# Attention and two MLPs on one core: the score buffer of queries 256 to 575 as two tiles of two banks, with a new table for the order

## The chip, the cores and the metric

The kernel runs on one core of a Trainium2 chip. The metric is the device time of one execution in microseconds. The engines are TensorE (PE; PEld are its weight loads), VectorE (DVE), ScalarE (ACT), GpSimd (POOL, nearly unused here) and SyncE (SP), whose queue issues every transfer. PE writes its products to PSUM, eight banks of 512 numbers per partition; DVE and ACT read them there.

## The reference

Three stages, all in 32-bit numbers. First causal attention by blocks of 64 (4 batches, 8 heads, 576 positions, 64 numbers per head):

```python
scores = scale * np.matmul(q, k.transpose(0, 1, 3, 2))
mask = block_i >= block_j
scores = np.where(mask, scores, -1000000000.0)
scores = scores - np.max(scores, axis=-1, keepdims=True)
attn = np.exp(scores)
attn = attn / (np.sum(attn, axis=-1, keepdims=True) + 1e-09)
return np.matmul(attn, v).astype(np.float32)
```

Its output is seen as 2304 tokens of 512 numbers. The first MLP is `h = x @ w_in` (512 to 2048), softplus, `g @ w_out` (2048 to 512). The second is `h = x @ w_in` (512 to 1024), h times softmax(h), a layer norm, and `ln @ w_out` (1024 to 512).

## The kernel before

**Precision.** Most operands are split into a high and a low part (`do_hi`/`do_lo`, `qk_hi`/`qk_lo`, `do_gh`/`do_gl`), and a product is three matmuls: high by high, high by low, low by high.

**Units of work.** `UnitA` (16 of them) is attention for queries 0 to 255 of one batch and two heads. `Piece` loads and splits one block of weights. `Pair` is two blocks of 128 hidden units of the first MLP for one chunk of 256 tokens: 24 matmuls into a tile `hp`, softplus on ACT and DVE (`abs`, `exp`, `ln`, `stt`, `do_gh`, `do_gl`), 24 matmuls into `acc`. `UnitC` (16 of them) is attention for queries 256 to 575 of one batch and two heads. `Tok` is the second MLP for 128 tokens (`h` and `op` are its matmul outputs).

**UnitC.** Its scores come in three parts: i = 0 (queries 256 to 383, 384 keys, two heads), i = 1 (queries 384 to 511, 512 keys, two heads) and i = 2 (the last 64 queries of both heads, 576 keys). They stand in one PSUM tile `S` of four banks: i = 0 in banks 0 and 1, i = 1 in banks 2 and 3, i = 2 again in banks 0 and 1 (`BANKS`, line 75). `mm_both` computes i = 0 and 1 in one go, `mm_qk(2)` comes when the exponentials of i = 0 are done. For each part `mask` writes the masked block (L466), `max` takes the row maximum (L471) and `exp` the exponentials with their sums (L480, one instruction per head). The exponentials are 32-bit; `split` copies their 16-bit halves apart (L243 on ACT, L245 on DVE), `tr` transposes them by a transfer (L511), and `merge` puts the halves together in `ps` (L521). `pv` multiplies `ps` with v into bank 3 of `S`; `scale` multiplies the result with the reciprocal sums (L537), and `x_hi`/`x_lo` (L243 or L245, L544) split it for the first MLP. `pv` and what follows of a unit are planned by `tail` while the next unit's scores are under way, so the product of unit n stands in the queues behind the scores of unit n+1.

**Order.** Every step is a task of a planner, `Plan`, with a duration, a rank and the tasks that it waits for; a task that can run on ACT or DVE names both. The planner lists the tasks engine by engine with a clock of its own; ranks are changed by the numbers in `OFF` (per step) and `RANK` (per kind of unit). The program is then emitted in that order and not reordered. Which semaphore waits an instruction gets is decided after that, from the tiles that it reads and writes. Every matmul but the transposes is recorded at L237.

Of the kernel before, what the change touches and what calls it, by code (L numbers as in the profile page):

```python
# [20 lines left out]


OFF = {
    "Pair.a": -30572.7, "Pair.abs": 25914.2, "Pair.b": -12790.1, "Pair.do_gh": -42748.1, "Pair.do_gl": -11944.0,
    "Pair.evac": -75046.1, "Pair.exp": -224132.0, "Pair.ln": -58821.8, "Pair.store": 28299.8, "Pair.stt": -51658.7,
    "Piece.bits0": -37390.9, "Piece.bits0@P0": 71539.5, "Piece.bits1": 159910.0, "Piece.bits1@P0": -41379.4,
    "Piece.do_hi": 106001.0, "Piece.do_hi@P0": 54788.8, "Piece.do_hi_g": -165029.0, "Piece.do_lo": 218994.0,
    "Piece.do_lo@P": -242194.0, "Piece.do_lo@P0": -14117.0, "Piece.do_lo_g": -38167.0, "Piece.load": 118853.0,
    "Piece.load@P0": -53132.4, "Piece.signed": 7535.9, "Piece.signed@P0": -56998.9, "Tok.a": -51047.8,
    "Tok.aggr": -41912.4, "Tok.bm": 27290.6, "Tok.center": -145283.0, "Tok.exp": 132540.0, "Tok.ln_hi": 136461.0,  # L30
    "Tok.ln_lo": 51440.0, "Tok.load": -208829.0, "Tok.logexp": -32647.3, "Tok.max": -40011.4, "Tok.merge": -254456.0,
    "Tok.mul": 16809.9, "Tok.o_evac": 16072.7, "Tok.small1": 16163.9, "Tok.small2": 138442.0, "Tok.split": 28685.9,
    "Tok.split_hi": -133834.0, "Tok.split_lo": -100488.0, "Tok.stats": -115234.0, "Tok.store": 248643.0,
    "Tok.tr": -134887.0, "Tok.x_hi": -156806.0, "Tok.x_lo": 115109.0, "UnitA.copy": -106614.0,
# [14 lines left out]
    "UnitC.den2": 150139.0, "UnitC.exp": 48708.5, "UnitC.load_qk": 26177.4, "UnitC.load_v": 7244.7,  # L49
    "UnitC.mask": -46322.9, "UnitC.max": -100744.0, "UnitC.merge": 34385.8, "UnitC.merge4": 216201.0,  # L50
    "UnitC.mm_both": -75275.5, "UnitC.mm_qk": 98914.6, "UnitC.norm": 45831.4, "UnitC.pv": 35917.7,
    "UnitC.qk_hi": -133419.0, "UnitC.qk_lo": -2441.9, "UnitC.rs_load": 47376.0, "UnitC.rs_store": -119437.0,
    "UnitC.scale": -84530.8, "UnitC.split": 35598.0, "UnitC.tr": -112828.0, "UnitC.x_hi": 94264.4,
    "UnitC.x_lo": -3061.1, "UnitC.xx": 34443.5,
}
RANK = {
# [4 lines left out]
}  # L61
MARGIN = {
    "PE": 600.0, "ACT": 100.0, "DVE": 100.0, "POOL": 100.0,
# [8 lines left out]

QA = (slice(0, 128), slice(128, 384))
MASKED = -8.0e9
BANKS = (slice(0, 2), slice(2, 4), slice(0, 2))

WC = (384, 512, 576)

# [149 lines left out]
def body(ctx: ExitStack, tc: tile.TileContext, qk, qkA, vP, vA, w1, w2, u1, u2, gln, out):  # L228
# [127 lines left out]
    class UnitC:  # L356
# [6 lines left out]
        def plan(self, prev, opened):  # L363
            p1, p2 = at_of(prev, len(prev) - 1), at_of(prev, len(prev) - 2)

            def g(u, *names):
                return [getattr(u, x) for x in names] if u else []

            self.t_qk = add("SP", dma_ns(128 * 3840), -12, self.load_qk, [opened] + g(p1, "t_ql"), DMA_LAT)
            self.t_qh = add({"ACT": act_ns(960), "DVE": dve_ns(960, .52)}, None, -6, self.qk_hi, [self.t_qk] + g(p1, "t_mm"))  # L370
            self.t_ql = add("DVE", dve_ns(960), -6, self.qk_lo, [self.t_qh])
            self.t_tr, self.t_mg, self.t_exp = [None, None, None], [[], [], []], {}
            mm01 = add("PE", 1614, 0.0, self.mm_both, [self.t_ql] + ([p1.t_exp[2, 0], p1.t_exp[1, 0]] if p1 else []) + g(p2, "t_xn"))
            for i, w in enumerate(WC):
                r, heads = 7.0 * i, ((0, 1), (1, 0), (0,))[i]
                if i < 2:
                    t = add("DVE", 140, r, partial(self.mask, i), [mm01])
                else:
                    self.t_mm = t = add("PE", 797, r, partial(self.mm_qk, 2), [mm01, self.t_exp[0, 0], self.t_exp[0, 1]])
                t = add("DVE", dve_ns(w * len(heads)), r, partial(self.max, i), [t])  # L380
                e = []
                for j in heads:
                    e.append(add("ACT", 250 + .833 * w, r, partial(self.exp, i, j), [t] + e + (p1.t_mg[i] if p1 else [])))
                    self.t_exp[i, j] = e[-1]
                if i == 1 and p1:
                    p1.tail([self.t_exp[1, 1]])
                cols, back = w * len(heads), [p1.t_tr[i]] if p1 else []
                n = [add({"ACT": 100 + .833 * cols, "DVE": 75 + .52 * cols}, None, r, partial(self.split, i, k), e + back) for k in range(2)]
                self.t_tr[i] = add("SP", 300 + 1.6 * cols, r, partial(self.tr, i), n, 2600.0)
            for i, w in enumerate(WC):  # L390
                r, cols = 7.0 * i + 4, w * (2 if i < 2 else 1)
                self.t_mg[i].append(add("DVE", 75 + 1.04 * cols, r, partial(self.merge, i), [self.t_tr[i]] + g(p1, "t_pv")))
                if i == 2:
                    self.t_mg[i] += [add({"ACT": 230, "DVE": 215}, None, r, partial(self.merge4, j), [self.t_tr[i]] + g(p1, "t_pv")) for j in range(2)]
            self.t_v = add("SP", dma_ns(327680), -8, self.load_v, [opened, self.t_qk] + g(p1, "t_pv", "t_v"), DMA_LAT)
            t = chain("DVE", 15, ((70, self.den0), (80, self.den1), (190, self.den2)), list(self.t_exp.values()) + g(p2, "t_rs"))
            self.t_rs = add("SP", 420, 15, self.rs_store, [t], 2400.0)
            self.t_rr = add("SP", 1000, 16, self.rs_load, [self.t_rs] + (p2.t_x if p2 else []), 2500.0)
            self.p1, self.group = p1, plan.group
            prev.append(self)  # L400
# [43 lines left out]

        def scores(self, i):

            return state["S"][:, BANKS[i], 0:WC[i] if i < 2 else WC[2] // 2]

        def mm_qk(self, i):
            S, w = self.scores(i), WC[i]  # L450
# [74 lines left out]
            copy(e, state["p4"].bitcast(U16)[64 * j:64 * j + 64].rearrange("p (q two) -> p q two", two=2), src)  # L525

        def pv(self):
            o, ps = state["S"][:, 3], state["ps"]
            for t in range(4):
                q0 = 0 if t < 3 else 128  # L530
                for j in range(2):
# [2 lines left out]

        def scale(self):
            self.xn = self.r
            DVE.tensor_mul(self.xn, state["S"][:, 3, 0:NB], self.r)  # L537

        def x_hi(self, c, off, done, w, e):
            copy(e, xt_of(c)[:, 0, self.pr, off:off + w], self.xn[:, done:done + w])  # L540
# [256 lines left out]
    def open_b():  # L797
# [1 line left out]
        right[0] = ExitStack()  # L799
        state["pat"] = right[0].enter_context(pool("atB", "right"))  # L800
        q = right[0].enter_context(pool("qaB", "right", space=PSUM))
        state["S"] = q.tile([128, 4, 512], F32, name="S")
        state["dC"] = [[state["pat"].tile([128, 32], F32, name=f"d{x}{i}") for x in "CT"] for i in range(2)]
        for d, _ in state["dC"]:
            DVE.memset(d, 1.0)
# [328 lines left out]
```

## Time and profile before

| | us |
|---|---|
| three runs, median (lowest, highest) | 785.98 (784.9, 786.38) |
| the profiled execution, its own time | 783.34 |
| its span from the first to the last instruction | 781.5 |
| PE busy, in the span | 734.6 |
| DVE busy, ACT busy | 577.6, 414.7 |

The span has three stages: UnitA with the weights up to 183.7 us, UnitC from there to about 440 us, and what is left of the first MLP with the second one up to the end. Pairs run beside all of the first two stages. The granted TensorE clock was 0.998 of the full 2.4 GHz in the mean.

### The profile page before, as it was taken

To read this page: it belongs to the slowest core of one execution; us is meant where nothing else is said; L and a number is where in the kernel's file an instruction comes from. 1 tells how busy PE (TensorE), PEld (TensorE's weight loads), DVE (VectorE), ACT (ScalarE), POOL (GpSimd) and SP (SyncE) were. 2 spreads that over 40 slices of the span, in tenths; PEclk is the share of its full clock that TensorE was granted. 3 is DMA by queue.
4 is the path that set the end of the run, shared out by engine and by line. 5 is a ranking of instruction groups with operands and counts; after the bars stand their busy time and mean duration, and the time that the engine had idled before them with its cause. 6 is when DMAs were issued, how large, how long until landed. Compare 5 with 4: busy or idle time off the path is not lost.

```text
span 781.5 us, 13790 instructions
## 1 busy us (share of the span) xinstructions
PE 734.6 (94%) x5336; PEld 654.3 (84%) x5336; DVE 577.6 (74%) x1219; ACT 414.7 (53%) x874; POOL 0.7 (0%) x6
## 2 busy tenths in 40 slices
PE   7799999999988888889879999999999999999998
PEld 5688889998777777778768999999999888888887
DVE  5998894367877788878867555424698999988882
ACT  5776765474557667766756455333463333323331
POOL 0000000000000000000000000000000000000000
PEclk9999999999999999999999999999999999999999
DMA  6754630212776777677676332002514443443323
GB/s 226 250 201 162 203 128 2 74 44 66 151 157 131 151 151 172 148 147 159 151 143 105 91 116 101 28 1 77 193 55 90 121 98 98 109 95 94 66 72 79
DMA packets 152673, 91.87 MB, mean 118 GB/s; under 512 B 122272, under 2 KB 135840, under 8 KB 152608
## 3 DMA queue, kind: packets, MB, share of 16 engines
q1 hardware_dynamic: 152608, 90.99, 46.0%
q8 instruction: 42, 0.69, 0.4%
q14 instruction: 23, 0.19, 0.1%
HBM read 51.91 MB, written 9.70 MB: 79 GB/s over the span
## 4 chain that ended last, share of the span: by engine, by line
PE 69%; DVE 14%; ACT 10%; DMA 4%; issue 3%; SPq 0%; ACTq 0%; DVEq 0%
PE hp L237 16%; PE acc L237 16%; PE op L237 13%; PE h L237 13%; PE S L237 8%; ACT eC L480 5%; DVE mC L471 4%; DMA raw<-in_w_dram 4%; PE R L237 2%; DVE a L314 2%; ACT hl L243 1%; DVE w L324 1%; DVE gl L758 1%; DVE t L750 1%; ACT t L741 1%
## 5 line engine op out<-in xcount | busy, mean ns | idle before, releaser
L237 PE MATMUL hp<-xt,w 128*128 128x256 f32 x1728 | 217.1, 281 | 0.1
L237 PEld LDWEIGHTS hp<-xt,w 128*128 128x128 f32 x1728 | 206.8, 189 | 6.3 <-issue 5.4
L237 PE MATMUL acc<-gh,w 128*128 128x256 f32 x768 | 146.3, 282 | 0.0
L237 PEld LDWEIGHTS acc<-gh,w 128*128 128x128 f32 x768 | 122.5, 190 | 2.9 <-issue 2.9
L237 PE MATMUL acc<-gl,w 128*128 128x256 f32 x384 | 107.7, 281 | 0.0
L237 PE MATMUL h<-u,w 128*128 128x512 f32 x432 | 100.6, 389 | 0.0
L237 PE MATMUL op<-w,w2w 128*128 128x512 f32 (+1 forms) x456 | 100.3, 378 | 0.0
L237 PEld LDWEIGHTS op<-w,w2w 128*128 128x128 f32 x456 | 82.5, 188 | 16.0
L237 PEld LDWEIGHTS h<-u,w 128*128 128x128 f32 x432 | 80.8, 188 | 16.5
L480 ACT ACTIVATE eC<-S,mC 128x384 f32<-128x384 f32 (+2 forms) x80 | 52.1, 653 | 72.5 <-DVE mC L471 28.6
L741 ACT ACTIVATE t<-hp 128x512 f32<-128x512 f32 x72 | 42.9, 596 | 83.7 <-PE hp L237 71.2
L750 DVE SCALAR_TENSOR_TENSOR t<-hp,t 128x512 f32<-128x512 f32 x72 | 49.3, 684 | 48.8 <-ACT t L747 47.9
L237 PEld LDWEIGHTS acc<-gl,w 128*128 128x128 f32 x384 | 72.6, 189 | 0.0
L471 DVE TENSOR_REDUCE mC<-S 128x2 f32<-128x768 f32 (+2 forms) x48 | 45.5, 975 | 9.1 <-ACT eC L480 5.0
L237 PE MATMUL S<-ps,v 128*64 128x320 f32 (+1 forms) x256 | 34.6, 412 | 18.6 <-DVE mC L471 14.2
L243 ACT ACTIVATE hl<-eC 128x576 uint16<-128x576 uint16 (+2 forms) x62 | 49.6, 829 | 0.8
L758 DVE TENSOR_TENSOR gl<-t,gh 128x512 fp32r<-128x512 f32 x72 | 49.1, 682 | 1.0 <-ACT gh L243 0.2
L237 PE MATMUL acc<-gh,w2w 128*128 128x256 f32 x256 | 48.4, 281 | 0.0
L744 ACT ACTIVATE t<-t 128x512 f32<-128x512 f32 x72 | 45.5, 633 | 1.5
L521 DVE COPY ps<-eC 128x1536 uint16<-128x1536 uint16 (+2 forms) x48 | 45.5, 947 | 1.1 <-DMA eC<-hl 1.0
L747 ACT ACTIVATE t<-t 128x512 f32<-128x512 f32 x72 | 45.3, 629 | 1.1
L237 PEld LDWEIGHTS S<-ps,v 128*64 128x64 f32 x256 | 16.9, 136 | 33.7 <-DVE mC L471 16.4
(173 smaller groups left out, 1050.0 us busy)
## 6 DMA issues: line engine op xcount, KB each, us to landing
raw<-in_w_dram SPq DMA_DIRECT2D x32, 512.0 KB, 4.3
qkC<-in_qk_dram SPq DMA_DIRECT2D x16, 480.0 KB, 4.0
raw_u<-in_u_dram SPq DMA_DIRECT2D x11, 512.0 KB, 3.5
v<-in_vP_dram SPq DMA_DIRECT2D x16, 320.0 KB, 3.1
x2s<-stg SPq DMA_DIRECT2D x18, 256.0 KB, 2.8
xr<-x2s SPq DMA_DIRECT2D x18, 256.0 KB, 3.2
qkA<-in_qkA_dram SPq DMA_DIRECT2D x16, 256.0 KB, 3.5
out_dram<-ob SPq DMA_DIRECT2D x15, 256.0 KB, 2.0
```

Source lines behind the costliest of these rows:

```text
L237: PE.matmul(out, lhsT, rhs, start=start, stop=stop, skip_group_check=True)
L243: ACT.activation(out, a, AF.Copy)
L314: DVE.scalar_tensor_tensor(out=self.a, in0=self.raw[:, :, 0], scalar=29, in1=self.a, op0=ALU.logical_shift_right, op1=ALU.bitwise_or)
L324: DVE.tensor_sub(self.lo, self.af, self.hi)
L471: DVE.tensor_reduce(out=self.m[:, i:4:2] if i < 2 else self.m[:, 4:5], in_=self.scores(i), axis=AX.X if i < 2 else AX.XY, op=ALU.max, nega ...
L480: ACT.activation(e, sc, AF.Exp, bias=self.m[:, c:c + 1], accum_out=self.den[:, d:d + 1])
L521: DVE.tensor_copy(dst, src)
L741: ACT.activation(self.t, self.hp, AF.Abs)
L744: ACT.activation(self.t, self.t, AF.Exp, scale=-1.0)
L747: ACT.activation(self.t, self.t, AF.Ln, bias=1.0)
L750: DVE.scalar_tensor_tensor(out=self.t, in0=self.hp, scalar=0.0, in1=self.t, op0=ALU.max, op1=ALU.add)
L758: DVE.tensor_sub(self.gl, self.t, self.gh)
```

## The change

The four-bank tile becomes two tiles of two banks, `S0` and `S1`. The banks are used as before: i = 0 and i = 2 in `S0`, i = 1 in `S1`, the product with v in the second bank of `S1`. `tail` of the unit before now hangs on the second exponential of i = 1 (head 0) and not on the first (head 1). All numbers in `OFF` and `RANK` are new (two rows of each are shown); the planner itself is the same.

```diff
 OFF = {
-    "Pair.a": -30572.7, "Pair.abs": 25914.2, "Pair.b": -12790.1, "Pair.do_gh": -42748.1, "Pair.do_gl": -11944.0,
+    "Pair.a": -37545.4, "Pair.abs": 40935.4, "Pair.b": -12936.9, "Pair.do_gh": -72836.8, "Pair.do_gl": 135125.0,
...
 RANK = {
-    "U2": (1044770.0, 6788.0), "Tok": (617171.0, 18564.5),
+    "U2": (1063100.0, 9138.15), "Tok": (672137.0, 5865.35),
...
-BANKS = (slice(0, 2), slice(2, 4), slice(0, 2))
...
                 if i == 1 and p1:
-                    p1.tail([self.t_exp[1, 1]])
+                    p1.tail([self.t_exp[1, 0]])
...
         def scores(self, i):
-            return state["S"][:, BANKS[i], 0:WC[i] if i < 2 else WC[2] // 2]
+            return state["S"][i % 2][:, :, 0:WC[i] if i < 2 else WC[2] // 2]
...
         def pv(self):
-            o, ps = state["S"][:, 3], state["ps"]
+            o, ps = state["S"][1][:, 1], state["ps"]
...
-            DVE.tensor_mul(self.xn, state["S"][:, 3, 0:NB], self.r)
+            DVE.tensor_mul(self.xn, state["S"][1][:, 1, 0:NB], self.r)
...
-        state["S"] = q.tile([128, 4, 512], F32, name="S")
+        state["S"] = [q.tile([128, 2, 512], F32, name=f"S{i}") for i in range(2)]
```

The lines below `BANKS` stand one line higher afterwards (L471 becomes L470). In the whole program DVE has 1241 instructions in place of 1219, and ACT 690 in place of 712 without the reads of sums; among what moved to DVE are 16 casts of `gh`. From the first mask of a UnitC to its last `scale` DVE has 427 in place of 414.

The first place is DVE in the middle of the UnitC stage, from the masks of one unit's scores to the maximum of i = 2 (128x1); the words in brackets name what an instruction waits for. Before:

```order
L466 MEMSET S_2238 64x2x64 [waits PE_49]
L466 MEMSET S_2238 64x2x64 [waits DVE_49]
L471 TENSOR_REDUCE mC_3152<-S_2238 128x2 [waits DVE_49]
L471 TENSOR_REDUCE mC_3152<-S_2238 128x2
L521 COPY ps_2252<-eC1_2246 128x2x4x256 [waits DMAHW2_49]
L245 COPY hl0_2248<-eC0_2245 128x768 [waits Activation_49]
L521 COPY ps_2252<-eC2_2247 128x8x128 [waits DMAHW4_49]
L750 SCALAR_TENSOR_TENSOR t_3132<-hp0_130,t_3132 128x512
L432 TENSOR_SCALAR qkh_3214<-qkC_3076 128x384 [waits DMAHW1_49,PE_49]
L433 CAST qkh_3214<-qkC_3076 128x576
L471 TENSOR_REDUCE mC_3152<-S_2238 128x1 [waits Activation_49]
```

The same stretch on DVE after the change, for the next unit but one:

```order
L465 MEMSET S0_2238 64x2x64 [waits PE_49]
L465 MEMSET S1_2239 64x2x64 [waits PE_49]
L470 TENSOR_REDUCE mC_3366<-S0_2238 128x2 [waits DVE_49]
L470 TENSOR_REDUCE mC_3366<-S1_2239 128x2 [waits DVE_49]
L520 COPY ps_2253<-eC2_2248 128x8x128 [waits DMAHW2_49]
L244 COPY hl0_2249<-eC0_2246 128x768 [waits Activation_49]
L244 COPY hl0_2249<-eC0_2246 128x768
L244 COPY hl1_2250<-eC1_2247 128x1024 [waits Activation_49]
L244 CAST gh_3424<-t_3282 128x512 [waits PE_49]
L757 TENSOR_TENSOR gl_3435<-t_3282,gh_3424 128x512 [waits DVE_49]
L470 TENSOR_REDUCE mC_3366<-S0_2238 128x1 [waits PE_49]
```

Each mask now waits for PE by itself, each maximum of i = 0 and 1 for its own mask, and the maximum of i = 2 for PE and no longer for ACT. The large merge has moved ahead of the masks; splits of i = 0 and a cast of `gh` stand where it was.

The second place is PE, from the scores of i = 2 (288 columns) over the product with v (`S<-ps,v`, `S<-p4,v`) to what follows it; `hp` are matmuls of a Pair. Before:

```order
L237 MATMUL S_2238<-qkh_3214 128x288 x2
L237 MATMUL S_2238<-qkl_3215,qkh_3214 128x288 x2
L237 MATMUL S_2238<-qkh_3214,qkl_3215 128x288 x2
L237 MATMUL hp1_131<-xt_2584,w1_2_99 128x256 x12
L237 MATMUL S_2238<-ps_2252,v_3298 64x320 x6
L237 MATMUL S_2238<-ps_2252,v_3298 64x192 x2
L237 MATMUL S_2238<-p4_2253,v_3298 128x64
L237 MATMUL hp1_131<-xt_2584,w1_3_100 128x256 x12
```

After, in a unit at about the same place:

```order
L236 MATMUL S0_2238<-qkh_3262 128x288 x2
L236 MATMUL S0_2238<-qkl_3263,qkh_3262 128x288 x2
L236 MATMUL S0_2238<-qkh_3262,qkl_3263 128x288 x2
L236 MATMUL S1_2239<-ps_2253,v_3325 64x320 x6
L236 MATMUL S1_2239<-ps_2253,v_3325 64x192 x2
L236 MATMUL S1_2239<-p4_2254,v_3325 128x64
L236 MATMUL hp0_130<-xt_2639,w1_4_101 128x256 x12
L236 MATMUL hp0_130<-xt_2639,w1_5_102 128x256 x12
L236 MATMUL S0_2238<-qkh_3437 128x384 x2
```

A product now writes `S1` and scores of i = 2 write `S0`. In every other unit nothing stands between them any more, and 48 in place of 36 matmuls of Pairs stand ahead of them; in the units between it is 36 and 12, as before everywhere. A unit has 72 matmuls of Pairs in its round in both orders.

## Rows read from the trace of the kernel before

**Rows 1.** The page: span; busy time and its share by engine.

```profile
span 781.5 us, 13790 instructions
PE 734.6 (94%) x5336; PEld 654.3 (84%) x5336; DVE 577.6 (74%) x1219; ACT 414.7 (53%) x874; POOL 0.7 (0%) x6
```

**Rows 2.** Windows (first column): length, busy of PE, PEld, DVE, ACT, POOL; clock; DMA.

```profile
0.00:183.70 183.70, 170.91 (x1450) 154.47 (x1450) 137.08 (x347) 115.90 (x283) 0.70 (x6) 1.00 0.42 140
183.70:440.00 256.30, 225.44 (x1799) 195.43 (x1800) 200.62 (x415) 166.30 (x361) 0.00 (x0) 0.99 0.68 142
440.00:778.25 338.25, 338.21 (x2094) 304.38 (x2088) 239.91 (x457) 131.99 (x230) 0.00 (x0) 1.00 0.33 87
285.58:316.31 30.73, 27.17 (x216) 23.23 (x217) 24.61 (x53) 21.46 (x47) 0.00 (x0) 1.00 0.72 164
```

**Rows 3.** Waits of PE, 184 to 440: who waited for whom; us, times, longest.

```profile
PE S L237 <- ACT eC L480: 15.5, 16, 3.0
PE S L237 <- DVE mC L471: 14.2, 11, 1.5
```

**Rows 4.** The chain that ended last, 284 to 332: start, us, what.

```profile
285.58 2.53 PE S L237 x18
...
292.51 0.18 DVE S L466
...
292.97 2.10 DVE mC L471 x2
...
295.14 0.67 ACT eC L480 x2
...
298.30 1.34 ACT eC L480 x4
...
299.67 0.77 DVE mC L471
...
300.48 2.53 PE S L237 x18
...
316.31 2.53 PE S L237 x18
```

**Rows 5.** Timeline, 284 to 304: start, us, engine, operation, idle before and releaser.

```profile
288.15 0.74 ACT L480 ACTIVATE eC<-S,mC 128x576 f32<-128x576 f32 x1 [2.32 <-PE S L237]
...
296.95 0.53 PE L237 MATMUL S<-qkh 128*128 128x288 f32 x2 [0.24 <-ACT eC L480]
...
297.85 0.28 PE L237 MATMUL acc<-gh,w2w 128*128 128x256 f32 x1
...
303.91 0.49 DVE L537 TENSOR_TENSOR rC<-S,rC 128x320 f32<-128x320 f32 x1 [1.75 <-ACT eC L480]
```

**Rows 6.** The chain that ended last, elsewhere: one block of a Pair; scores.

```profile
290.99 1.44 PE S L237 x12
...
446.34 2.83 PE acc L237 x24
```

**Rows 7.** Groups by line and shape: the cast of `gh` on either engine.

```profile
L245 DVE CAST gh<-t 128x512 fp32r<-128x512 f32 x43 | 18.2, 423 | 7.0 <-PE acc L237 4.9 <-PE R L237 1.7
...
L243 ACT ACTIVATE gh<-t 128x512 fp32r<-128x512 f32 x29 | 18.1, 625 | 3.9 <-PE acc L237 2.3 <-DVE t L750 1.3
```

**Rows 8.** Waits of DVE, 285.58 to 316.31: us, times, longest.

```profile
DVE rC L537 <- ACT eC L480: 1.7, 1, 1.7
DVE hl L245 <- ACT eC L480: 1.4, 2, 0.7
DVE dC L483 <- ACT eC L480: 1.1, 1, 1.1
...
DVE S L466 <- PE S L237: 0.5, 1, 0.5
```

**Rows 9.** Timeline of SP: the large transpose of one unit: start, us.

```profile
302.02 3.58 SPq L511 DMA_TRANSPOSE eC<-hl  x1
```

**Rows 10.** Window after PE's longest wait: length, PE busy, clock, DMA, GB/s.

```profile
405.00:410.00 5.00, 2.81 (x12) 0.72 0.81 98
```

More of the change, by code (lines that the diff above doesn't have):

```diff
@@ L23 @@
 OFF = {
-    "Pair.a": -30572.7, "Pair.abs": 25914.2, "Pair.b": -12790.1, "Pair.do_gh": -42748.1, "Pair.do_gl": -11944.0,
[L25 to L33, printed above, removed]
@@ L34 @@
-    "Tok.tr": -134887.0, "Tok.x_hi": -156806.0, "Tok.x_lo": 115109.0, "UnitA.copy": -106614.0,
[14 rows of a table removed]
[L49 to L52, printed above, removed]
@@ L53 @@
-    "UnitC.scale": -84530.8, "UnitC.split": 35598.0, "UnitC.tr": -112828.0, "UnitC.x_hi": 94264.4,
-    "UnitC.x_lo": -3061.1, "UnitC.xx": 34443.5,
+    "Pair.a": -37545.4, "Pair.abs": 40935.4, "Pair.b": -12936.9, "Pair.do_gh": -72836.8, "Pair.do_gl": 135125.0,
+    "Pair.evac": -93303.3, "Pair.exp": -316321.0, "Pair.ln": -123958.0, "Pair.store": 107773.0, "Pair.stt": -122013.0,
+    "Piece.bits0": -120438.0, "Piece.bits0@P0": 52621.5, "Piece.bits1": 181314.0, "Piece.bits1@P0": -143932.0,
+    "Piece.do_hi": 33368.4, "Piece.do_hi@P0": 70703.9, "Piece.do_hi_g": -185387.0, "Piece.do_lo": 235970.0,
@@ new lines @@
+    "Piece.do_lo@P": -118806.0, "Piece.do_lo@P0": -27399.0, "Piece.do_lo_g": -50436.8, "Piece.load": 36413.1,
+    "Piece.load@P0": -128957.0, "Piece.signed": 5116.0, "Piece.signed@P0": -100737.0, "Tok.a": 33835.4,
+    "Tok.aggr": -75143.4, "Tok.bm": 59440.3, "Tok.center": -177401.0, "Tok.exp": 181567.0, "Tok.ln_hi": 131112.0,
+    "Tok.ln_lo": 181302.0, "Tok.load": -53477.9, "Tok.logexp": 12672.8, "Tok.max": -34572.9, "Tok.merge": -212570.0,
+    "Tok.mul": 52009.8, "Tok.o_evac": 6503.8, "Tok.small1": 26265.5, "Tok.small2": 115389.0, "Tok.split": 52428.6,
@@ new lines @@
+    "Tok.split_hi": -116208.0, "Tok.split_lo": -45030.4, "Tok.stats": -120555.0, "Tok.store": 273298.0,
+    "Tok.tr": -180588.0, "Tok.x_hi": -303336.0, "Tok.x_lo": 122175.0, "UnitA.copy": -146385.0,
[15 rows of a table added]
+    "UnitC.load_v": -52247.9, "UnitC.mask": -71623.0, "UnitC.max": -32195.3, "UnitC.merge": 57206.2,
+    "UnitC.merge4": 277967.0, "UnitC.mm_both": -120703.0, "UnitC.mm_qk": 74970.8, "UnitC.norm": 20902.1,
+    "UnitC.pv": 1130.5, "UnitC.qk_hi": -132619.0, "UnitC.qk_lo": -7691.7, "UnitC.rs_load": 55613.1,
@@ L55 @@
+    "UnitC.rs_store": -192882.0, "UnitC.scale": -143539.0, "UnitC.split": 86408.4, "UnitC.tr": -166925.0,
+    "UnitC.x_hi": 126479.0, "UnitC.x_lo": -18102.3, "UnitC.xx": 68623.1,
 }
 RANK = {
[4 rows of a table removed]
[4 rows of a table added]
 }
```

35 rows, old and new, of tables (OFF, RANK) are left out of this document.

## Prediction

> **What bounds the kernel now.** I read the page first, then windows by stage, PE's waits in the stage where it idles, and the chain and timeline of one round there. PE is busy for 94% of the span [rows 1], and the windows show where the rest is [rows 2]: from 440 us to the last matmul it never pauses, in the first 183.7 us it idles 12.8, and in the UnitC stage 256.30 - 225.44 = 30.9. So the work is bound by PE, and only what removes idle time of PE can save anything; the UnitC stage holds most of it. Nearly all of that is waits of the score and product matmuls: 15.5 us for exponentials and 14.2 for maxima [rows 3]. The second number is the odd one: a product with v needs bank 3 free of exponentials, not a maximum.
>
> The round of two units shows it. From product to product (300.48, next but one 285.58 to 316.31) it takes 30.73 us [rows 4], and PE idles 30.73 - 27.17 = 3.56 of it [rows 2]. Follow one unit from the end of the scores at 290.99 + 1.44 = 292.43 [rows 6]: masks, both maxima (2.10, one after the other), only then the first exponential at 295.14, the exponentials of i = 1 up to 299.64, then the maximum of i = 2 (0.77), and only behind that the product at 300.48 [rows 4]. That is 8.05 us. PE has 36 matmuls of Pairs at 2.83 / 24 each (4.24), the scores of i = 2 (296.95 to 297.85, 0.90) and 12 more (1.41) to put beside it [rows 5, 6]: 6.55. The 1.5 us between them is the bubble of this unit. The exponential of i = 2 then waits 2.32 for the product, and the scaling of the product 1.75 for that exponential [rows 5]. Banks 0 and 1 and banks 2 and 3 run as one queue, although their data don't depend on each other in these places.
>
> A page's reading of busy time bears on the 3.56. The Trainium skill, Perfetto Trace Analysis, section "Identifying the Most-Contended Engine", holds that busy time of matmuls tells little about headroom, since they overlap. The trace agrees: by starts, two units are 144 x 2.83 / 24 + 2 x (1.44 + 0.90 + 2.53) = 26.7 us [rows 4 to 6], under the 27.17 shown as busy. By busy time the 15 intervals between 16 units would hold 7.5 x 3.56 = 26.7 us, by starts 7.5 x 4.0 = 30.
>
> **The change, part by part.**
> *Two tiles.* No bank, matmul or byte is added. The order with its waits shows what goes: the maximum of i = 2 waits for PE, not for ACT. So the product need not come behind that maximum, nor the exponential of i = 2 behind the product, nor the scaling behind the exponential. The first exponential can start after the first maximum: 2.10 us split by columns, 768 to 1024, are 0.90 and 1.20. What is late next, counted from the end of the scores: masks 0.54 (292.43 to 292.97), first maximum 0.90, the exponentials of i = 0 at 0.67 each: 2.8; PE comes to the scores of i = 2 after 36 or 48 matmuls, 4.24 or 5.65. The second maximum is done at 2.64, the exponentials of i = 1 (1.34) then at 4.1, or 4.7 with another ACT operation of 0.6 between them; PE comes to the product at 6.55 in both kinds of unit. So these waits end 1.4 to 1.9 us before PE asks.
>
> *New waits.* The product waits for both exponentials of i = 1 (that is the 4.7), the first score matmul of the next unit for the exponential of i = 2, and the first one into `S1` for the scaling. In the second stretch of DVE shown, the maximum of i = 2 stands behind a split that waits for the last exponential, a cast, a `gl`: about 4.7 + 0.7 + 0.4 + 0.7 + 0.8 = 7.3, its exponential ends about 8.1, and the next unit's scores come at 6.55 + 2.53 + 2.83 = 11.9. The scaling (0.49) has 24 matmuls and half of the scores, 3.5 us. Behind a waiting score matmul stands all of PE's queue; by these margins none waits. I price them at 0; if a margin were gone they would cost what they do now, 1.5 a unit.
>
> *New order on DVE.* This is the unknown. DVE is busy 24.61 us in a round [rows 2], 0.46 for each of its 53 instructions, and the stage gets 13 more: 6.0 us, 0.8 a round. So DVE has 25.4 us of work in a round that PE could do in 26.7, and its own waits must fit into 1.3. Today it has 6.1 (30.73 - 24.61). Those for the scaling and for the maximum of i = 2 come from the shared tile; those of the splits (1.4), the sums `dC` (1.1) and the masks (0.5) are real dependences [rows 8], 3.0 together, which a round may hide or not. With none of them left the round is PE's 26.7; with all of them 25.4 + 3.0 = 28.4. I take 27.1, nearer the lower end, since the order now has other work ahead of those splits and the masks wait apart. That saves 30.73 - 27.1 = 3.6 a round, 7.5 x 3.6 = 27.
>
> *Ends of the stage.* The first and last units have rounds of their own, in which the transposes of the first unit must still land before its product; I take 2.5 us off, between 0 and one round's 4.
>
> *The clock.* After PE's longest wait (3.0 us, [rows 3]) the granted clock fell to 0.72 over 405 to 410 us [rows 10], that is to 1.2 GHz for a part of it, at a loss of 5.00 x 0.28 = 1.4 us. Without a wait that long it should stay at 2.4 GHz: 1.4 us saved, or 0 if a wait of this length remains.
>
> *The other stages.* PE's order is the same up to its 29th block, and both other stages only trade places of equal blocks. Moving 16 casts of `gh` costs DVE 16 x 0.42 = 6.8 us and frees ACT of 16 x 0.63 [rows 7]; after 440 us PE is at work without a gap while DVE has 239.91 of 338.25 [rows 2], which hides it. What it costs without that cover is its own length. In the first stage DVE has 137.08 of 183.70; I take 0, with 2 either way.
>
> *Sum.* 27 - 2.5 + 1.4 = 25.9 us less than the profiled execution's 783.34, so 757.4. The median of the runs lies 2.64 above that execution; on its scale the forecast is **760.0**.
>
> **Rivals.**
> *DVE takes over.* The round becomes 28.4 as above: 2.3 x 7.5 = 17.5 us saved, no clock term, 783.34 - 17.5 + 2.64 = 768.5. For it: 25.4 of 26.7 is tight for a queue in order. Against: DVE's waits have been spread by the shared tile, and a late DVE has 1.4 to 1.9 us before PE notices.
>
> *No gain.* The bubble stays because it is one of PSUM space, or because the transposes take its place: the large one held SP for 3.58 us behind the load of the next q and k [rows 9], and SP's new order puts the loads of v and of q and k ahead of the third transpose in every other unit. One more such hold in a round makes it 26.7 + 3.6 = 30.3, 3 us saved in all: 783 to 786. The Trainium skill, Perfetto Trace Analysis, section "Optimization Strategy", speaks for this side: bubbles that repeat in a stretch can mean too little PSUM or SBUF for the next tile, and this change adds none, so by it the time would stay at 786. The trace doesn't bear it out: what released the product was a maximum over other banks, not a bank that came free [rows 3, 4].
>
> *Slower.* DVE's added work lands in the round and its waits stay what they are: 25.4 + 6.1 = 31.5, 0.8 more than now, 7.5 x 0.8 = 6 us, 792. The place is DVE's queue between the masks and the maximum of i = 2: an instruction there that waits for ACT (the split of i = 1) holds up that maximum and all behind it. It decides from 30.73 - 25.4 = 5.3 us of waits in a round. Against it: 3.0 of the 6.1 are all that real dependences explain.
>
> That the change doesn't do what it says is excluded by the order: the wait for ACT is gone.
>
> **How the numbers follow.** The forecast's own case (rounds of 26.7 to 27.6, 2 us either way outside the stage: 753 to 764) gets 0.66, DVE taking over (764 to 776) 0.20, no gain 0.04, slower 0.05; 0.05 is left for a gain beyond the first case (new order better in the first stage too). All of the 4.0 in each round and the clock would be 30 + 1.4, 754.6, and with 2 us from the first stage 752.6. The range is 752.5 to 771: it leaves out half of the second case's upper part, the two last ones and the extreme gain, together about 0.18. Runs of this kernel tell 0.2% (1.6 us) from no change; faster by more than that are the first two cases and the last, 0.91, same 0.04, slower 0.05.
>
> **What would show it.** After the change PE's idle time between its first UnitC score and the last product should be under 6 us, with a round of two units near 27 from product to product; no wait of a product for a maximum; exponentials of i = 2 that start before the product ends; DVE busy above 90% of a round. The UnitC stage should end about 25 us earlier and everything behind it should run as before, without a gap. The forecast is wrong if rounds are over 28, if PE waits for `gl` or `ps` in place of `S`, or if gaps appear after the UnitC stage.

## The result and the profile after

The changed kernel takes 747.26 us (median of four runs, 743.83 to 747.67) against 786.05 for the kernel before (784.9 to 786.38): ratio 0.950, 95% interval 0.947 to 0.953. The forecast was 760.0 with a range of 752.5 to 771; the direction and the mechanism were right, the gain was 38.8 us where 26 were forecast, and the time lies 5.2 us below the range. The profiled execution takes 747.20 us with a span of 745.4, 36.1 less than before. Below, a unit's "scores" are those of i = 0 and 1.

The page: span and busy time, to be held against [rows 1].

```profile
span 745.4 us, 13779 instructions
PE 728.6 (98%) x5336; PEld 651.4 (87%) x5336; DVE 587.7 (79%) x1241; ACT 399.9 (54%) x852; POOL 0.7 (0%) x6
```

Windows, with the columns of [rows 2]: the first stage, the UnitC stage up to 0.41 us behind the start of its last product (where the row of before ends too), the rest, and one round of two units.

```profile
0.00:184.50 184.50, 172.12 (x1460) 155.48 (x1460) 139.82 (x352) 113.37 (x280) 0.70 (x6) 1.00 0.41 139
184.50:410.94 226.44, 225.36 (x1847) 198.64 (x1848) 202.75 (x424) 159.14 (x356) 0.00 (x0) 1.00 0.75 161
410.94:742.20 331.26, 331.14 (x2034) 297.31 (x2028) 245.14 (x465) 127.01 (x217) 0.00 (x0) 1.00 0.34 90
330.67:357.13 26.46, 26.46 (x219) 23.02 (x220) 25.25 (x53) 20.64 (x47) 0.00 (x0) 1.00 0.73 168
```

The UnitC stage is 256.30 - 226.44 = 29.9 us shorter and holds 48 matmuls more than before. At 2.83 / 24 us each [rows 6] these are 5.7 us, which the stages beside it no longer hold: the last one is 7.0 shorter with 60 matmuls less, which is 7.1, so nothing was won there. In the first stage 10 more matmuls (1.2) took 0.8 longer. The gain is therefore 29.9 + 5.7 = 35.5 in the UnitC stage and 0.4 in the first.

PE's waits over 184.5 to 413 us, the answer to [rows 3].

```profile
PE S L236 <- ACT eC L479: 1.0, 1, 1.0
```

One wait of 1.0 us is left of 29.7. The chain of waits over one round of two units, against [rows 4]; columns as there.

```profile
330.67 2.46 PE S L236 x18
333.13 2.88 PE acc L236 x24
336.01 1.42 PE S L236 x11
337.43 2.94 PE hp L236 x24
340.37 2.73 PE acc L236 x24
343.09 3.25 PE S L236 x24
...
357.13 2.46 PE S L236 x18
```

DVE and ACT have left the chain: it is PE without a break, 26.46 us from product to product in place of 30.73. That is less than the 27.17 which the same work counted as busy in a round of before [rows 2]. One matmul of a Pair is shown as 0.28 us long [rows 5] but 24 of them take 2.83 [rows 6]: each shown end lies past the next start, and ahead of a wait this end counts as busy time. Only distances from start to start show what PE needs.

The timeline of the unit whose scores end at 337.43 (one with 48 matmuls of Pairs ahead of the scores of i = 2): start, us, engine, line, operation; in brackets the idle time before it.

```profile
338.44 0.31 DVE L465 MEMSET S<- 64x128 f32 x2
338.66 2.06 DVE L470 TENSOR_REDUCE mC<-S 128x2 f32<-128x768 f32 x2
...
339.68 0.58 ACT L479 ACTIVATE eC<-S,mC 128x384 f32<-128x384 f32 x1 [0.32 <-issue]
...
341.97 0.68 ACT L479 ACTIVATE eC<-S,mC 128x512 f32<-128x512 f32 x1
...
342.93 0.43 PE L236 MATMUL S<-qkh 128*128 128x288 f32 x2
...
343.82 2.16 PE L236 MATMUL S<-ps,v 128*64 128x320 f32 x16
...
344.45 0.75 DVE L470 TENSOR_REDUCE mC<-S 128x1 f32<-128x576 f32 x1
...
345.60 0.74 ACT L479 ACTIVATE eC<-S,mC 128x576 f32<-128x576 f32 x1
```

The first exponential starts in the middle of the two maxima. The last one of i = 1 ends at 342.65, and PE reaches the product 1.2 us later. The product starts before the maximum of i = 2, and the exponential of i = 2 starts inside the product. These are the three things that the one tile forbade. The place where nothing stands between the scores of i = 2 and the product, as here, comes less often than in "every other unit": by the starts of the matmuls in four units, and in two more the product stands ahead of these scores.

The waits of DVE in this round, against [rows 8], and the groups of the cast of `gh`, against [rows 7].

```profile
DVE hl L244 <- ACT eC L479: 0.5, 1, 0.5
DVE dC L482 <- ACT eC L479: 0.3, 1, 0.3
```

```profile
L244 DVE CAST gh<-t 128x512 fp32r<-128x512 f32 x59 | 24.9, 422 | 11.9 <-PE acc L236 8.8 <-PE R L236 2.8
...
L242 ACT ACTIVATE gh<-t 128x512 fp32r<-128x512 f32 x13 | 8.2, 631 | 5.6 <-PE acc L236 3.4 <-DVE t L749 2.1
```

### The profile page after: what moved, and what is told of

It is laid out like the page before. It is cut to its first block, busy times and chain, and to the rows that moved or that the text cites. A ratio compares the mean times of both kernels' runs of the same rounds, so it can differ in the third digit from the quotient of the medians.

```text
span 745.4 us, 13779 instructions
## 1 busy us (share of the span) xinstructions
PE 728.6 (98%) x5336; PEld 651.4 (87%) x5336; DVE 587.7 (79%) x1241; ACT 399.9 (54%) x852; POOL 0.7 (0%) x6
## 4 chain that ended last, share of the span: by engine, by line
PE 83%; DVE 9%; DMA 4%; ACT 3%; issue 1%; SPq 0%; ACTq 0%; DVEq 0%
PE hp L236 22%; PE acc L236 21%; PE op L236 13%; PE h L236 13%; PE S L236 9%; PE R L236 3%; DVE a L313 2%; DMA raw<-in_w_dram 2%; DMA eC<-hl 2%; DVE w L323 1%; ACT eC L479 1%; DVE mA L621 1%; PE r L236 1%; DVE gl L757 1%; DMA qkA<-in_qkA_dram 1%
## 5 line engine op out<-in xcount | busy, mean ns | idle before, releaser
L1050 ACT ACTIVATE ob<-op,A 128x512 f32<-128x512 f32 (+1 forms) x19 | 12.7, 667 | 60.3 <-PE op L236 56.4
L470 DVE TENSOR_REDUCE mC<-S 128x2 f32<-128x768 f32 (+2 forms) x48 | 44.9, 961 | 0.0
L236 PEld LDWEIGHTS acc<-gh,w2w 128*128 128x128 f32 x256 | 40.4, 189 | 1.4 <-issue 1.1
L242 ACT ACTIVATE hl<-eC 128x1024 uint16<-128x1024 uint16 (+2 forms) x48 | 40.5, 863 | 0.4
```

Of the source, the lines that this page charges most:

```text
L236: PE.matmul(out, lhsT, rhs, start=start, stop=stop, skip_group_check=True)
L242: ACT.activation(out, a, AF.Copy)
L470: DVE.tensor_reduce(out=self.m[:, i:4:2] if i < 2 else self.m[:, 4:5], in_=self.scores(i), axis=AX.X if i < 2 else AX.XY, op=ALU.max, nega ...
L1050: ACT.activation(self.ob[:, cols], self.o[cols.start][:, cols], AF.Copy, scale=self.A)
```

## The experiments

All ratios are to the kernel before, run beside it on the same chip; brackets hold the 95% interval. Runs on different chips are compared by these ratios.

### Is it the tiles or the order? (e1, e2, e9, e10)

e1 keeps the new order and joins the two tiles again:

```diff
-        state["S"] = [q.tile([128, 2, 512], F32, name=f"S{i}") for i in range(2)]
+        S4 = q.tile([128, 4, 512], F32, name="S")
+        state["S"] = [S4[:, 0:2], S4[:, 2:4]]
```

> The kernel after with its new order on every engine, but with the scores and the product with v again in one tile of four banks (same banks, same instructions, same order; only the waits differ). Theory A, the tile makes the gain: the product again waits for the maximum of i = 2, which now stands right in front of it, and every exponential for both maxima; the bubble of 1.5 us or more a unit is back, round of two units 30 us or more, 780 to 800 us. Theory B, the order makes the gain: the round stays near 26.5 us and the time at 747 to 753. Theory C, each half of the change does a part: 762 to 775.

Measured: 784.34 us, 0.9985 [0.9966, 1.0003]. The new order alone is worth nothing that can be told from noise. PE's waits in its UnitC stage:

```profile
PE S L236 <- ACT eC L479: 26.6, 16, 3.0
PE S L236 <- DVE mC L470: 1.7, 5, 0.5
```

The sum is nearly that of [rows 3], 28.3 for 29.7, but the names have changed places: in this order the maxima release almost none of it. Which engine a wait is put down to says who came last, not what costs the time.

e2 is the other half, the old order with the edit of the tiles (the `scores`, `pv`, `scale` and allocation lines of the diff, nothing else):

> The kernel before with its old order on every engine, but with the two tiles of two banks. Theory A: the waits for ACT and for the maxima go without any new order; the first exponential starts after the first maximum, exponentials of i = 1 are done 4.1 to 4.7 us after the scores while PE comes to the product after 6.55; round of two units 26.5 to 27.6 us, PE idle under 8 us in the UnitC stage, 752 to 762 us. Theory B: no gain from the tiles alone, round 30 us or more, 782 to 788. Theory C, DVE in its old order comes too late for the scores of the next unit: round 28 to 29.5, 764 to 776.

Measured: 749.99 us, 0.9547 [0.9525, 0.9569]. The tiles alone bring almost all of it, more than Theory A's 752 to 762. The stage and one round of e2, columns of [rows 2]:

```profile
184.00:411.00 227.00, 224.47 (x1839) 197.48 (x1838) 196.85 (x417) 167.82 (x364) 0.00 (x0) 1.00 0.77 163
281.82:308.30 26.48, 26.48 (x219) 23.07 (x220) 24.00 (x54) 21.34 (x47) 0.00 (x0) 1.00 0.89 191
```

A round is 26.48 us, PE without a break, as in the changed kernel. e9 and e10 set the two side by side on one chip.

> The changed kernel itself, on one chip with the old order and two tiles (e10), to tell what the new order adds to the two tiles. Theory A (the tiles make the whole gain; the profiled spans were 745.4 and 745.0): the two differ by under 0.3%. Rival: the new order is worth 0.3 to 0.7%, 2.5 to 5 us, since it has an idle PE for 1.1 us in the UnitC stage where the old order has 2.5 and wider margins in some units.

> The old order with two tiles once more, beside e9. Theory A: within 0.3% of e9. Rival: 2.5 to 5 us slower than e9.

Measured: 747.27 us, 0.9508 [0.9489, 0.9528], and 750.70 us, 0.9566 [0.9542, 0.9589]. The new order adds 3.4 us on top of the tiles by the medians, 0.6% by the ratios; Theory A's 0.3% fell. The profiled executions do not show where: their spans are 746.3 and 746.9 here, 745.4 and 745.0 in the first runs of the two. That stays open.

### How do the waits of one tile make 35 us? (e5 to e8, e13, e14)

These start from e2 (the old order, two tiles) and put the lost waits back one at a time, by exchanging the two maxima or by writing an unused number into the bank of the product. In e2 a unit looks like this (timeline; its scores end at 288.58):

```profile
293.78 0.71 ACT L480 ACTIVATE eC<-S,mC 128x512 f32<-128x512 f32 x1
...
294.37 0.75 DVE L471 TENSOR_REDUCE mC<-S 128x1 f32<-128x576 f32 x1
294.99 2.16 PE L237 MATMUL S<-ps,v 128*64 128x320 f32 x16
295.56 0.73 ACT L480 ACTIVATE eC<-S,mC 128x576 f32<-128x576 f32 x1
```

The product starts 0.5 us behind the last exponential of i = 1 (294.49), and 0.13 before the maximum of i = 2 is done (295.12).

e5, the first exponential behind both maxima:

```diff
         def max(self, i):
...
+            i = (1, 0, 2)[i]
             DVE.tensor_reduce(out=self.m[:, i:4:2] if i < 2 else self.m[:, 4:5], ...
```

> Old order, two tiles (as the run e2), and the two maxima of a unit change places on DVE (that of i = 1 first), so that the first exponential comes behind both again, as it did with one tile. In e2 the exponentials of i = 1 end 5.6 to 5.9 us after the scores of a unit and PE comes to the product after 6.42. Theory A (links of one chain, each priced by what it eats of that margin): exponentials of i = 0 end at about 4.0 (scores of i = 2 at 4.14, no wait), those of i = 1 at 6.7 to 7.0, the product 0.3 to 0.6 late: 5 to 10 us over e2, 755 to 760. Rival: the first exponential's wait was what mattered, 770 or more. Rival: covered by the Pairs, no change, 749 to 752.

Measured: 764.66 us, 0.9758 [0.9734, 0.9781], 2.0% over e2 and e10 (0.9557 in the mean), some 16 us. This is between Theory A and its first rival; the mechanism is Theory A's, the price higher. The timeline of one unit:

```profile
289.37 0.58 ACT L481 ACTIVATE eC<-S,mC 128x384 f32<-128x384 f32 x1 [1.94 <-DVE mC L472]
...
293.10 0.68 ACT L481 ACTIVATE eC<-S,mC 128x512 f32<-128x512 f32 x1
...
293.92 2.16 PE L237 MATMUL S<-ps,v 128*64 128x320 f32 x16 [0.31 <-ACT eC L481]
```

ACT sits 1.94 us before the first exponential, the last one of i = 1 ends at 293.78, and the product waits for it.

e6, the product behind the maximum of i = 2:

```diff
+            if i == 2:
+                DVE.memset(state["S"][1][0:64, 1, 511:512], 0.0)
```

(behind the maximum, in `max`)

> Old order, two tiles, and DVE writes one unused number per partition of the product's bank right behind the maximum of i = 2, so that the product with v waits for that maximum again, as with one tile. In e2 that maximum ends 6.53 us after the scores and PE comes to the product after 6.42. Theory A: 0.2 to 0.3 us a unit, 3 to 5 us over e2, 753 to 755: the wait that the profile of before names (14.2 us for maxima) is only the last link, not the cause. Rival: this wait is the bubble itself and comes back in full, 0.9 to 1.5 us a unit, 764 to 774.

Measured: 756.81 us, 0.9657 [0.9622, 0.9692], about 8 us, between the two theories. The direct wait for it is small:

```profile
PE S L237 <- DVE S L473: 3.9, 12, 1.7
PE S L237 <- ACT eC L482: 2.7, 2, 1.8
```

e7, the exponential of i = 2 behind the product:

```diff
+            if i == 2:
+                ACT.activation(state["S"][1][0:64, 1, 510:511], self.m[0:64, 4:5], AF.Copy)
             ACT.activation(e, sc, AF.Exp, ...
```

> Old order, two tiles, and ACT writes one unused number per partition of the product's bank right ahead of the exponential of i = 2, so that this exponential waits for the product again and the scaling of the product for ACT, as with one tile. It adds an ACT instruction of about 0.2 us a unit and holds ACT for some 2.3 us in each unit; ACT has about 20 of 26.5 us of work in a round of two units. Theory A: ACT's exponentials of the next unit come later, part of it shows: 753 to 762. Rival: ACT has room for it, 750 to 752. Rival: this link alone brings the bubble back, 775 or more.

Measured: 753.56 us, 0.9610 [0.9581, 0.9640], about 4 us, at the lower edge of Theory A. The interval touches that of e10, so this price is the least certain of the three. e8 has all three edits.

> Old order, two tiles, with the three links of e5, e6 and e7 together: nearly all of the waits of one tile, but in two tiles. Theory A (the links make one ring, scores, both maxima, exponentials, product, exponential of i = 2, scaling, next scores, and only together do they outlast the Pairs): more than the sum of the three singly, 775 to 786. Rival, they add up: 764 to 772. Rival, something else in the one tile costs the 35 us: under 762.

Measured: 773.64 us, 0.9873 [0.9849, 0.9897], about 25 us, a little less than the sum of the three (16 + 8 + 4) and between the two ranges. So they add up, roughly; Theory A's "more than the sum" fell. Some 10 us of the 35 were missing, and e13 put back the two waits that e8 had left out: the write of e6 also ahead of the maximum of i = 2, and the write of e7 also behind the exponential of i = 2 (columns 509 and 508).

> As e8, with two more links: DVE writes an unused number per partition of the product's bank also right ahead of the maximum of i = 2, so that this maximum stands behind the exponentials of i = 1, and ACT writes one also behind the exponential of i = 2, so that the scaling of the product stands behind that exponential. These are the waits that the one tile had and e8 left out. Theory A (the one tile costs what its waits cost, and these two are the 10 us that e8 lacks): 780 to 788. Rival (the missing 10 us have another cause, not a wait): 773 to 777.

Measured: 783.44 us, 0.9978 [0.9965, 0.9992]. All but 0.2% of the loss is back, with two tiles and the old order. A round in the chain of waits of e13:

```profile
252.23 2.53 PE S L237 x18
...
282.94 2.53 PE S L237 x18
```

30.71 us from product to product, where before has 30.73 [rows 4]. So these five waits are enough to make the round of before. The four writes are work too, 0.12 us on DVE and 0.32 on ACT in each unit, and no run has them without the waits. In a round they are 0.9 us long, so even if all of that lay in the ring most of the 4 us would be the waits'. The timeline shows the last of the waits, the counterpart of [rows 5]:

```profile
301.08 0.15 ACT L489 ACTIVATE S<-mC 64x1 f32<-64x1 f32 x1
301.27 0.49 DVE L546 TENSOR_TENSOR rC<-S,rC 128x320 f32<-128x320 f32 x1 [1.96 <-ACT S L489]
```

DVE idles 1.96 us before the scaling, and the masks and maxima of the next unit stand behind it in DVE's queue. e14 took one of the two alone, the maximum of i = 2 behind the exponentials of i = 1, on top of e6.

> As e6, with the maximum of i = 2 behind the exponentials of i = 1 as well, and nothing else. In e2 these exponentials end 5.6 to 5.9 us after the scores, so the maximum ends at 6.5 to 6.8 and the product, at 6.42 in e2, starts at about 6.9. Theory A: 0 to 3 us over e6, 755 to 760, since DVE came to this maximum at 5.8 to 5.9 anyway; the link matters only where another one has made the exponentials late. Rival: it is the link that was missing, by itself worth the 10 us: 764 to 769.

Measured: 760.39 us, 0.9689 [0.9662, 0.9717], 0.3% over e6 with overlapping intervals: as Theory A had it, this link alone is worth little. The other one, the write behind the exponential of i = 2, was not run alone.

### How near is DVE? (e3, e4, e11, e12)

e3 takes the hanging of `tail` back (`p1.tail([self.t_exp[1, 1]])` for `[1, 0]`).

> The kernel after with one number of the change taken back: the tail of the unit before hangs on the exponential of i = 1, head 1, as it did before, not on head 0. The planner then puts four matmul blocks and the product in another sequence in some units. Theory A (the two tiles leave 1 to 2 us of slack ahead of every score and product matmul, so a small shift in the order costs nothing): 747 within 0.5%, 744 to 751. Theory B (the order is finely tuned and the hanging matters): over 753, with waits of PE for DVE or ACT in the UnitC stage.

Measured: 754.21 us, 0.9600 [0.9579, 0.9621]: Theory B. In the order that results, five units in place of two have the product ahead of the scores of i = 2, so that less of PE's work stands between the scores and it, and in four of them PE waits 0.6 to 1.8 us for exponentials. The numbers of the table fit one hanging. The waits of PE over the stage, and the longest one:

```profile
PE S L236 <- ACT eC L479: 6.1, 8, 1.8
```

```profile
398.69 2.16 PE L236 MATMUL S<-ps,v 128*64 128x320 f32 x16 [1.79 <-ACT eC L479]
```

e4 and e11 add two and four copies a unit on DVE to the changed kernel:

```diff
         def mask(self, i):
             DVE.memset(self.scores(i)[0:64, :, WC[i] - 64:WC[i]], MASKED / 8)
+            if i == 1:
+                for _ in range(2):
+                    DVE.tensor_copy(state["xx"][:, 1], state["xx"][:, 0])
```

> The kernel after with two copies of 128x512 on DVE added in every UnitC, right behind the second mask and ahead of the maxima, the same order otherwise; about 0.85 us of DVE a unit, 13.5 us in the stage, where DVE has 204 of 228.5 us at work. Theory A (DVE has slack of 1 us or more a unit before PE notices): 747 to 750. Theory D (DVE is the bound in the changed kernel already, as the second rival had it): each copy is paid in full or nearly, 757 to 761.

> As e4, but four copies of 128x512 a unit in place of two, 1.7 us, 27 us in the stage, on top of 204 us that DVE works there in 228.5. Two copies cost about 8 of their 13.5 us. Theory D (from there on DVE is the bound): the two further copies are paid in full, 13.5 more, 766 to 771. Rival (only lateness of single maxima, with DVE's waits as a reserve): again some 60%, 760 to 765.

Measured: 754.55 us, 0.9610 [0.9580, 0.9639], and 767.59 us, 0.9780 [0.9759, 0.9801]. Against e9 (0.9508) the first two copies cost 1.0%, 8 of their 13.5 us, and the next two 1.7%, 13.4 of 13.5: Theory D for the second step. By the intervals either price holds within some 3 us. The UnitC stage of e4 and of e11, columns of [rows 2]:

```profile
184.50:421.50 237.00, 230.43 (x1873) 201.55 (x1873) 216.69 (x462) 159.76 (x356) 0.00 (x0) 1.00 0.71 155
```

```profile
184.50:434.00 249.50, 233.02 (x1881) 202.84 (x1881) 230.90 (x496) 159.53 (x357) 0.00 (x0) 1.00 0.69 148
```

DVE is busy for 91.4% and 92.5% of them (89.5% in the changed kernel); it never reaches the full time, and still the second step is paid in full. The copies also stand ahead of the maxima, so they could cost time merely as links between the scores and the exponentials. Then one would expect DVE to wait for PE's scores in each unit. In e11 it does so three times in the stage, and its other waits are for transposes and for ACT:

```profile
DVE ps L523 <- DMA eC<-hl: 5.5, 6, 1.4
DVE hl L244 <- ACT eC L482: 2.5, 5, 0.7
...
DVE S L465 <- PE S L236: 2.1, 3, 1.0
```

So DVE is behind PE there, and PE waits for it by way of the exponentials, 15.8 us in the stage. In e12, the same two copies stand in the old order.

> The old order with two tiles and two copies of 128x512 a unit added at the same place as in e4. In the old order the masks and maxima of the middle units begin 0.9 us sooner after their scores than in most units of the new one and DVE has 196.5 us of work in the stage instead of 204. Theory A (what counts is how late DVE is at the masks): 3 to 6 us over e10. Rival (the products have only 0.5 to 0.8 us of margin in the old order, and the copies push the exponentials back by 0.85): 8 to 13 us over e10.

Measured: 755.25 us, 0.9626 [0.9598, 0.9653], 0.6% over e10: Theory A, 4.7 us of 13.5. That is less than the 8 of the new order, but the two prices differ by no more than their noise, and the times themselves are about equal (0.9626 and 0.9610). That the old order leaves DVE more room is likely and not shown.

## Why the prediction was wrong in size

**What held.** PE bound the kernel, the 4 us in each round were a ring of waits made by the shared tile, and the tiles open it (e1, e2, e13). The steps of a unit came out near their forecast: the last exponential of i = 1 ended 5.2 us after the scores (forecast 4.1 to 4.7), PE came to the product at 6.4 (6.55), so that 1.2 us of margin were left (1.4 to 1.9), the exponential of i = 2 ended at 8.9 (8.1), the next scores came at 11.7 (11.9). DVE has 25.25 us of work in a round (25.4). The moved casts of `gh` went from 43 to 59 on DVE and cost nothing that shows. The granted clock of the profiled execution is 1.000, with no fall like the 0.72 of before, as the clock term said. That fall had cost 1.7 us (forecast 1.4): behind the wait of 2.98 the scores of i = 2 took 1.81 in place of 0.90, and 12 matmuls of a Pair 2.20 in place of 1.41 (the chain of before).

```profile
407.19 1.81 PE S L237 x6
409.00 2.20 PE acc L237 x12
```

**The step that failed first: "I take 27.1".** A round measured 26.46. Of the difference, 0.24 lies in the floor of 26.7: its terms were durations of groups in the chain, which hold the modelled end of their last matmul, and that overlaps what follows (a product takes 2.46 of the chain now, 2.53 then). The other 0.4 was kept back for DVE, since 3.0 us of its waits counted as real dependences that a round may not hide. They were not a fixed amount. The waits for exponentials in [rows 8] fell from 1.4 and 1.1 to 0.5 and 0.3, and it is not the new order that did it: in the round of e2, with the old order, both are gone. These are all the waits of DVE in that round:

```profile
DVE S L466 <- PE S L237: 1.3, 2, 0.8
DVE rC L537 <- ACT t L741: 0.8, 1, 0.8
```

So these waits came from the ring that delayed the exponentials, and went with it. Over 7.5 rounds, all taken as the one shown, the step is (30.73 - 26.46) x 7.5 = 32.0 in place of 27, 5 us short.

**"I take 2.5 us off" for the ends.** The stage as a whole gave 35.5, the regular rounds 32.0 of them. Ends and clock together gave 3.5 where -2.5 + 1.4 = -1.1 stood, 4.6 short; with the clock at 1.7, the ends gave 1.8. No row asked for that deduction: the waits of [rows 3], 29.7 us, included those of the first and the last units, and the sum was built from regular rounds alone.

**The 2.64 us between the profiled execution and the median.** It was carried over unchanged; now it is 0.06. This part is luck. One profiled execution is a single draw: over the runs of this document the median lies from 2.5 us below it (e1) to 4.4 above it (e13), and in e2 it lies 3.2 above although the waits are gone there too. A lower clock goes with some of the scatter: of the runs of before that stand beside the experiments, the six with a granted clock of 0.990 or 0.991 took 786.1 us in the mean, the 15 with 0.996 to 0.998 took 784.3. The profiled execution of before had 0.998.

These three make 5.0 + 4.6 + 2.6, and with the 0.4 of the first stage 12.6 of the 12.7 us. The lower bound, 752.6, had 4.0 us a round where 4.27 came, gave the ends nothing and carried over the 2.64, so the range ended above the result.

**The rivals.** DVE did not take over, but it is next: two copies more in each unit cost 8 us, and the next two were paid in full (e11). "No gain" by a shortage of PSUM did not come: the Trainium skill, Perfetto Trace Analysis, section "Optimization Strategy", says that repeated bubbles can point to too little buffer space. Here the trace does not agree, 29.7 us of them went to 1.0 with the same four banks. "Slower" rested on DVE keeping its 6.1 us of waits; 1.2 are left in the round shown (26.46 - 25.25).

**The new order** was priced as an unknown on DVE's side. It is worth 3.4 us of the 38.8, and the runs do not show why: with the copies added the two orders take the same time (e4, e12), so more room on DVE's side is not what they bear out.

## What to carry to other kernels

Where independent parts of a computation share one tile, look in the trace for waits whose two ends touch different banks; making them separate tiles cost no memory here and gave 4.5% with the order unchanged. To price such an edit, sum the idle time of the whole stage by starts of matmuls, and ask of each wait on another engine whether it sits in the same ring: those of DVE for exponentials did, and shrank with it. The engine that a wait names is the last in the ring: e1 lost the same 28 us to other names.

## What was not expected of the hardware

A stage can be bound by an engine that is 92% busy: in e11 DVE's 0.85 us a unit beyond e4 came out at full price within the noise, with 18.6 us of idle time left on DVE in the stage (249.50 - 230.90), of which it waited 2.1 for PE. And PE's busy share misled in the other direction: 27.17 us counted as busy in a round of 30.73 became 26.46 without a gap.
